# Handing out VectorE's work between pieces: attention's masked copies and transposes, the sums of x, one silu product, and the rows of the output tile

## Chip, core and metric

The kernel runs on one core of one Trainium2 chip. The metric is the device time of one execution in microseconds (us). TensorE does the matrix products, VectorE (DVE in the profile) and GpSimd (POOL) the elementwise work, ScalarE (ACT) activations and copies, and SyncE (SP) issues most of the transfers. Each engine works its own instructions in the order in which the program issues them. Between engines, semaphores hold an instruction back until what it reads has been written and what it overwrites has been read.

## What is computed

Two stages follow each other. The first is a linear attention with a decay per channel; the second is a feed-forward layer with a silu gate.

```python
for t in range(S):                                   # r, k, v: (4, 8, 768, 48)
    cur = einsum('bhd,bhe->bhde', u[None] * kt, vt)
    y[:, :, t] = einsum('bhd,bhde->bhe', rt, state + cur)
    state = w[None, :, :, None] * state + einsum('bhd,bhe->bhde', kt, vt)
x = y.transpose(0, 2, 1, 3).reshape(3072, 384)
g, val = x @ w_gate, x @ w_val                       # (3072, 1536)
out = (g * (1 / (1 + exp(-g))) * val) @ w_out        # (3072, 384)
```

## The kernel before

The sequence is cut into blocks of 128 tokens: 24 blocks (`N`), four of them (one for each batch) at every one of six places in time. Attention of block `i` is done in chunked form. `turn_blocks` puts k and r with the channel on partitions, by two VectorE transposes, first k (`kT`), then r (`rT`). Before it `move_blocks` has brought the 32x32 blocks into place by 16 transfers on SP's queue; these overwrite what the transposes of the block before read, so they wait for its second transpose. `scores` multiplies the two on TensorE for even and odd heads, and two `copy_predicated` (L392) put the upper triangles into `At`. `outputs` forms the rows of x, `update` the state. The main loop over `s` (L1036) does `scores(s-1)`, `outputs(s-2)`, `update(s-2)` and `turn_blocks(s)`; from `s = 12` on the transposes are VectorE's.

Between these parts of attention stand five gaps. In each, `feed(n)` takes `n` pieces of the feed-forward layer from the list `todo`. A piece issues a few TensorE products and the VectorE, ScalarE and GpSimd work that belongs to them. So the order of the work on every engine is written out by the program: what is issued at one place in the loop stands at one place in every engine's queue.

The feed-forward layer has two shapes after the first two pairs of blocks. Pair `g` is two blocks (256 tokens).

- `three_beside(g)`, for g = 2, 4 and 6, makes gate and value products of pairs g and g+1 with 15 products of sums where 18 plain ones would be needed. It runs over t = 0 to 3, three columns of 128 of the weights each. The 15 steps of one t are called r0 to r14 and numbered 0 to 14 in `BESIDE` (`ENDING` for t = 3); step n of t has the time 15 t + n. One step is two matmuls of 256 columns (L710). Steps collect in chains, each in a PSUM bank; a chain that is read out (L735) between two of its steps must be read before the next one adds to it. Of the six results of one t, three are gates, in rows of the tile `hv`, and three are values, in the last six rows of `hv` (`NR` and on, the same rows for every t). `silu` activates a gate (L742) and multiplies it by its value (L735, `hv<-hv`): product i = 0 and 1 of a t on VectorE early in the next t, i = 2 on GpSimd.
- `two_projections(g)` projects pairs g and g+1 with seven products of half size each, named by pair and number: "00" to "06", "10" to "16" (L529, six matmuls of 192 columns each). Before them stand sums of h (`h_sums`, L503 to L507). One of the items also issues eleven VectorE sums of x (`x_forms`, L668 to L678), which the next `three_beside` or `three_units` reads. The items come in the order 00 10 01 02 11 04 03 12 05 06 13 14 15 16. The results go to `o_sb1` and `o_sb2`, two buffers each, by copies and sums (L535 to L545), and from there to `out` by transfers that ScalarE issues (L553).

`queue` mixes the two: the first three pieces of the next `three_beside` (steps r10, r14, r12, each of which opens a chain and takes a free bank) are put between the last projections, in the order 13, r10, 14, r14, 15, r12, 16. Project "15" ends with the ScalarE copy (L539) that frees the bank which r12 takes. The last four pairs use `three_units` (g = 8 and 10), after attention.

Of the kernel before, what the change touches and what calls it, by code (L numbers as in the profile page):

```python
# [15 lines left out]
P = 128  # L16
# [6 lines left out]
def fast(  # L23
# [57 lines left out]
    NX = 10  # L81
    xT = cst.tile([P, NX, CC, P], FP32, name="xT")
    NR = 2 * FC
    hv = cst.tile([P, NR + 6, 2 * P], FP32, name="hv")
    hTs = hv[:, 0:NR].rearrange("p (j f) t -> p j f t", j=2)
    sgs = cst.tile([P, 3, 2 * P], FP32, name="sgs")
    free_sg = deque(sgs[:, n] for n in range(3))
# [287 lines left out]
    def turn_blocks(i):  # L375

        turned[i] = three.tile([P, HP, P], FP32, name="rT", tag="rT")
        for dst, src in ((kT[i % 2], blocks[0]), (turned[i], blocks[1])):
            dve.transpose(dst[:].rearrange("p a t -> p (a t)"), src)

    def scores(i):

        ps = [ps_a.tile([P, HP, P], FP32, name="s_ps", tag="a") for _ in range(2)]
        for a in range(HP):
            for e in range(2):
                rows = slice(64 * e, 64 * e + D)
                pe.matmul(  # L387
                    ps[e][:, a, :], kT[i % 2][rows, at(i, a), :], turned[i][rows, at(i, a), :],
                    start=True, stop=True, skip_group_check=True,
                )  # L390
        for e in range(2):
            dve.copy_predicated(  # L392
                At[i % 2][:].rearrange("p (a e) t -> p a e t", e=2)[:, :, e],
                mask[:].bitcast(INT32).unsqueeze(1).to_broadcast([P, HP, P]), ps[e][:],
            )

    def outputs(i):

# [110 lines left out]
    def project(g, n):  # L509

        h11, h12, h21, h22 = h_quarters(g)
        x = part_of.setdefault(g, {})
        if n == 0:
            assert done["pool"] == NW
            if g == 0:
                free.extend(banks[2:])
            x["a"] = take()
            x["out"] = [two.tile([P, DM], FP32, name=n, tag=n) for n in ("o_sb1", "o_sb2")]
        if n == 1:
            x["b"] = take()  # L520
        lhs, rhs, acc = (
            (h11, w11, "a"), (h12, w21, "b"), (1, wt[0], "a"), (2, wt[1], "a"),
            (0, w12, "b"), (h22, wt[2], "a"), (3, w22, "b"),
        )[n]
        if isinstance(lhs, int):
            lhs = x["s"][lhs]
        ps = x[acc][:, 0:NH]
        for f in range(FH):
            pe.matmul(  # L529
                ps, lhs[:, f, :], rhs[:, f, :],  # L530
                start=(f == 0 and n in (0, 1, 4)), stop=(f == FH - 1), skip_group_check=True,
            )
        o1, o2 = x["out"]
        if n in (0, 2, 3):
            act.copy({0: o1[:, 0:NH], 2: o1[:, NH:DM], 3: o2[:, NH:DM]}[n], ps)  # L535
        elif n == 1:
            dve.tensor_add(o1[:, 0:NH], o1[:, 0:NH], ps)
        elif n == 5:
            act.copy(o2[:, 0:NH], ps)  # L539
            free.append(x["a"])  # L540
        elif n == 6:
            dve.tensor_add(o1[:, NH:DM], o1[:, NH:DM], ps)  # L542
        if n in (3, 4):
            if "c22" in x:
                dve.tensor_add(o2[:, NH:DM], o2[:, NH:DM], x["b"][:, 0:NH])  # L545
            x["c22"] = True
        if n == 6:
            free.append(x["b"])
        if n >= 5:
            j = 6 - n  # L550
            c, b = divmod(2 * g + j, B)
            n0 = S * b + P * c
            act.dma_start(out=out[n0 : n0 + P, :], in_=x["out"][j][:])  # L553

# [14 lines left out]
    def two_projections(g):  # L569

        def item(j, p):
            if g >= FIRST and (j, p) == (0, 1):
                for do in wide.pop("last"):
                    do()
            if (j, p) in ((1, 0), (0, 1)):
                h_sums(g, p)
            elif (j, p) in ((1, 1), (0, 3)):
                h_sums(g + 1, p // 3)
            elif g + 2 < THREES and (j, p) == (0, 6):
                x_forms(g + 2)  # L580
# [27 lines left out]
    wide, todo_forms = {}, deque()  # L608

    def in_place(t):  # L610

# [42 lines left out]
    def x_forms(g):  # L654

        (x00, x01), (x10, x11), (x20, x21) = x_halves(g)
        lows2 = [two.tile([P, 3, 2, P], FP32, name="xf", tag="w_low") for _ in range(2)]
        v = [t[:, n] for t in lows2 for n in range(3)]
        if g < THREES:
            v += [sgs[:, n].rearrange("p (i t) -> p i t", i=2) for n in range(3)] + [x01, x10]  # L660
        else:
            last = two.tile([P, H, D], FP32, name="xf", tag="rk")
            v += [
                t.rearrange("p h d -> p (h d)")[:, 0 : 2 * P].rearrange("p (i t) -> p i t", i=2)
                for t in [x[:] for x in r_ld + k_ld] + [last[:]]
            ]
        v10, v13, v6, v2, v12, d1, v3, v1, v8, v4, v14 = v
        dve.tensor_add(v10, x01, x21)  # L668
        dve.tensor_sub(v13, x00, v10)
        dve.tensor_add(v12, v13, x20)  # L670
        dve.tensor_sub(d1, x11, x10)
        dve.tensor_sub(v2, d1, x20)
        dve.tensor_add(v6, v2, x21)
        dve.tensor_sub(v3, x00, x11)
        dve.tensor_sub(v1, x10, x00)
        dve.tensor_sub(v8, x01, x11)
        dve.tensor_sub(v4, x01, x00)
        dve.tensor_add(v14, x10, x20)  # L678
        wide["v", g] = {
            "r0": d1, "r1": v1, "r2": v2, "r3": v3, "r4": v4, "r5": x00, "r6": v6, "r7": x21,  # L680
            "r8": v8, "r9": x20, "r10": v10, "r11": x11, "r12": v12, "r13": v13, "r14": v14,
        }

    def prepare_threes(g, n):
        if g >= THREES and n == 10:
            x_forms(g)
        if g > THREES:
            return
        if n == 1:
            if g == FIRST:  # L690
# [34 lines left out]
    def three_beside(g):  # L725

        todo = []
        values = hv[:, NR : NR + 6].rearrange("p (j i) t -> p j i t", j=2)

        def pair_of(x):  # L730
            return x.rearrange("p (o t) -> p o t", o=2)
# [13 lines left out]
        for t in range(4):  # L745
# [8 lines left out]
            if t < 3:  # L754
                forms = w_forms(g, t + 1)
                if g == FIRST and t < 2:
                    forms += in_place(t + 2)
                start = z - 4 if t else 0
                todo += [
                    (start + (z + 10 - start) * n / len(forms) + 0.15, do)  # L760
                    for n, do in enumerate(forms)
                ]
            gates = [[j * FC + 3 * t + i for i in range(3)] for j in range(2)]
            c = []
            for k in range(6):
                i, j = divmod(k, 2)
                row, other = gates[j][i], NR + 3 * j + i
# [30 lines left out]
            if t < 3:  # L798
                for i, on in enumerate((dve, dve, pool)):
                    silu(  # L800
                        *((z + 11.7, z + 11.8) if i == 2 else (z + 15.6 + i / 10, z + 16.2 + i / 10)),
                        hTs[:, :, 3 * t + i], values[:, :, i], on,
                    )
            else:
# [99 lines left out]
    def feed(n, pops=1):  # L904
        for _ in range(n):
            ready = [k for k, (need, _) in enumerate(todo) if need <= done["pool"] + len(summed)]
            if ready:
                todo.pop(ready[0])[1]()
            for _ in range(min(pops, len(small))):
                small.popleft()()  # L910

    def queue(g):
# [5 lines left out]
        elif g % 2 and g > 1:  # L918
# [593 lines left out]
```

## Time and profile before

| what | value |
|---|---|
| median of 3 runs | 608.4 us (608.32 to 608.64) |
| the profiled execution | 608.25 us |
| its span (first to last instruction) | 606.5 us |
| TensorE busy | 587.9 us (97% of the span) |
| VectorE busy | 408.4 us (67%) |
| GpSimd busy | 311.6 us (51%) |
| ScalarE busy | 228.2 us (38%) |
| mean granted TensorE clock | 0.999 |

The span and the time differ by 1.75 us, which lie outside the first and the last instruction. The busy share of TensorE counts matmuls to their modelled ends, which overlap: matmuls of 256 columns start 0.216 us apart and are shown about 0.38 us long. A step of `three_beside` (four rows in the records, since each fp32 matmul appears twice) therefore takes 0.86 us, and one of the seven products of a projection (12 rows) 1.95 us; a wait is best read as what two starts lie apart beyond that.

### The profile page before, as it was taken

What the parts mean: (1) busy time and instruction counts of PE and PEld (TensorE: products, weight loads), DVE (VectorE), ACT (ScalarE), POOL (GpSimd) and SP (SyncE); (2) the same over time, 40 slices, a digit from 0 to 9 for tenths busy, and PEclk for the clock granted to TensorE, in tenths of its full rate; (3) what the DMA queues carried; (4) which work ended last, traced back from release to release, by engine and by line L of the source; (5) the groups of instructions that cost most, each with busy time, mean ns of one, the idle gap of its engine ahead of it and who ended that gap; (6) DMA issues with size and microseconds to landing.
All of it is one profiled execution on the core that took longest, in us unless ns stands there. A gap on an engine that the chain in (4) does not pass through costs nothing.

```text
span 606.5 us, 12429 instructions
## 1 busy us (share of the span) xinstructions
PE 587.9 (97%) x4920; PEld 527.2 (87%) x4920; DVE 408.4 (67%) x682; ACT 228.2 (38%) x524; POOL 311.6 (51%) x349
## 2 busy tenths in 40 slices
PE   8799999999999999999999999999999999999996
PEld 7588888899888899888799988889888899988896
DVE  6767877369478876478778377868537674377660
ACT  3358887330453422154331233432233420243310
POOL 4779879988999402967701866632435300001000
PEclk9999999999999999999999999999999999999999
DMA  6979883241530503133151404131100000100001
GB/s 168 237 210 245 221 294 77 46 70 31 123 49 9 93 5 72 42 60 56 21 85 21 96 3 67 19 51 24 37 17 1 1 0 19 35 1 1 2 1 57
DMA packets 138004, 40.43 MB, mean 67 GB/s; under 512 B 128592, under 2 KB 131792, under 8 KB 137936
## 3 DMA queue, kind: packets, MB, share of 16 engines
q1 hardware_dynamic: 134480, 34.82, 27.2%
q10 hardware_dynamic: 3456, 4.72, 2.2%
q8 instruction: 41, 0.67, 0.5%
q14 instruction: 27, 0.22, 0.1%
HBM read 28.51 MB, written 4.72 MB: 55 GB/s over the span
## 4 chain that ended last, share of the span: by engine, by line
PE 83%; DVE 4%; POOL 3%; ACT 2%; issue 1%; DMA 1%; ACTq 0%; DVEq 0%; SPq 0%; POOLq 0%
PE bank L710 27%; PE bank L529 26%; PE bank L455 7%; PE c_l L710 6%; PE y_ps L417 5%; PE c_n L710 3%; PE c_y L710 3%; PE s_ps L387 3%; DVE hv L735 2%; POOL wgv L222 1%; PE u_ps L432 1%; PE tp L349 1%; DMA r_ld<-in_r_dram 1%; ACT hv L735 1%; ACT hv L742 1%
## 5 line engine op out<-in xcount | busy, mean ns | idle before, releaser
L735 DVE TENSOR_TENSOR hv<-hv,bank 128x512 f32<-128x512 f32 x132 | 87.5, 681 | 29.8 <-PE bank L710 16.8
L455 PE MATMUL bank<-xT,wgv 128*128 128x256 f32 x288 | 66.8, 385 | 0.6 <-ACT xT L421 0.6
L710 PE MATMUL bank<-xf,wgv 128*128 128x256 f32 x256 | 65.9, 382 | 1.1 <-ACT o_sb L539 1.1
L328 ACT ACTIVATE At<-ident,du 128x128 f32<-128x128 f32 x176 | 60.1, 396 | 14.8 <-DVE o_sb L542 6.9
L849 POOL TENSOR_TENSOR hv<-At,hats 128x512 f32<-128x512 f32 x8 | 10.2, 1274 | 107.0 <-ACT At L848 107.0
L735 ACT COPY hv<-bank 128x512 f32<-128x512 f32 x72 | 40.3, 585 | 58.2 <-PE bank L710 43.4
L455 PEld LDWEIGHTS bank<-xT,wgv 128*128 128x128 f32 x288 | 53.2, 190 | 8.9 <-ACT xT L421 0.8
L710 PEld LDWEIGHTS bank<-xf,wgv 128*128 128x128 f32 x256 | 48.0, 190 | 8.6 <-ACT o_sb L539 1.8
L642 POOL TENSOR_TENSOR s<-wgv 128x256 f32<-128x256 f32 x39 | 29.3, 773 | 43.3 <-PE bank L529 43.3
L529 PE MATMUL bank<-wo,hv 128*128 128x192 f32 x288 | 49.5, 327 | 0.0
L529 PEld LDWEIGHTS bank<-wo,hv 128*128 128x128 f32 x288 | 47.3, 190 | 0.5
L392 DVE COPY_PREDICATED At<-mask,s_ps 128x512 f32<-128x512 int32 x48 | 33.1, 744 | 19.1 <-ACT At L328 10.5
L445 POOL TENSOR_TENSOR Z<-Z,w 48x192 f32<-48x192 f32 x32 | 17.3, 540 | 53.3 <-DVE Z L444 52.0
L529 PE MATMUL bank<-wo,hs 128*128 128x192 f32 x240 | 42.5, 327 | 1.2 <-DVE o_sb L545 1.2
L529 PE MATMUL bank<-wt,hs 128*128 128x192 f32 x240 | 42.1, 328 | 0.1
L535 ACT COPY o_sb<-bank 128x192 f32<-128x192 f32 x36 | 11.3, 315 | 80.2 <-PE bank L529 70.6
L529 PEld LDWEIGHTS bank<-wo,hs 128*128 128x128 f32 x240 | 39.6, 190 | 1.9 <-DVE o_sb L545 1.5
L529 PEld LDWEIGHTS bank<-wt,hs 128*128 128x128 f32 x240 | 39.2, 190 | 1.1 <-issue 0.7
L710 PE MATMUL bank<-xT,s 128*128 128x256 f32 x152 | 36.4, 383 | 2.5 <-DVE hv L735 2.0
L742 ACT ACTIVATE hv<-hv 128x512 f32<-128x512 f32 (+1 forms) x33 | 21.2, 668 | 45.2 <-DVE hv L735 45.2
L417 PE MATMUL y_ps<-At,v_ld 128*32 128x128 f32 x768 | 34.9, 273 | 1.4 <-DVE At L392 1.4
L710 PE MATMUL bank<-xT,wgv 128*128 128x256 f32 x144 | 35.9, 382 | 0.0
(212 smaller groups left out, 1302.0 us busy)
## 6 DMA issues: line engine op xcount, KB each, us to landing
hats<-hats SPq DMA_DIRECT2D x192, 32.0 KB, 2.0
w_bits<-in_moe_w_gate_dram SPq DMA_DIRECT2D x6, 768.0 KB, 6.7
v_ld<-in_v_dram SPq DMA_DIRECT2D x48, 96.0 KB, 3.5
w_bits<-in_moe_w_val_dram SPq DMA_DIRECT2D x6, 768.0 KB, 6.1
w_bits<-in_moe_w_out_dram SPq DMA_DIRECT2D x6, 768.0 KB, 7.1
out_dram<-o_sb ACTq DMA_DIRECT2D x24, 192.0 KB, 1.9
k_ld<-in_k_dram SPq DMA_DIRECT2D x20, 192.0 KB, 3.4
r_ld<-in_r_dram SPq DMA_DIRECT2D x20, 192.0 KB, 3.8
```

The lines of the kernel that those rows point to most:

```text
L328: lambda h=h: act.activation(At[i % 2][:, h, :], ident[:], AF.Identity, scale=du[:, h : h + 1])
L387: pe.matmul(ps[e][:, a, :], kT[i % 2][rows, at(i, a), :], turned[i][rows, at(i, a), :], start=True, stop=True, skip_group_check=True,)
L392: dve.copy_predicated(At[i % 2][:].rearrange("p (a e) t -> p a e t", e=2)[:, :, e], mask[:].bitcast(INT32).unsqueeze(1).to_broadcast([P, H ...
L417: pe.matmul(ps[32 * q : 32 * q + 32, cc, :], *x, start=start, stop=stop, skip_group_check=True,)
L445: pool.tensor_mul(ze, ze, w)
L455: pe.matmul(gv[:, o, :].rearrange("p (i t) -> p i t", i=2), wt[:, c, P * f : P * (f + 1)], xT[:, 2 * g % NX : 2 * g % NX + 2, c, :], start ...
L529: pe.matmul(ps, lhs[:, f, :], rhs[:, f, :], start=(f == 0 and n in (0, 1, 4)), stop=(f == FH - 1), skip_group_check=True,)
L535: act.copy({0: o1[:, 0:NH], 2: o1[:, NH:DM], 3: o2[:, NH:DM]}[n], ps)
L642: op(made[o], made[a], made[b])
L710: pe.matmul(ps[:, o], u[:, o], v, start=first and o == 0, stop=True, skip_group_check=True,)
L735: do(out, *(pair_of(wide[a][:]) if isinstance(a, str) else a for a in args))
L742: todo.append((at, lambda: act.activation(gate, gate, AF.Silu)))
```

## The change

1. Of the two masked copies of `scores`, for blocks from 12 on, only the first is issued at once. The second is put in a list `lazy`, and the next `feed` issues it behind its first piece.
2. `turn_blocks` issues one piece between the transpose of k and that of r. To make up for it the gap ahead of it (gap 1) feeds one piece less.
3. The eleven sums of x are made into a list, two of which go into each of six items of `two_projections`, from "03" to "14" (before: all eleven in item "06" or, for the sums of pairs 8 and on, "13"). Their order changes a little.
4. Product i = 1 of t = 0 and 1 is issued at step 7.1 of the next t instead of 1.3.
5. The values of t = 1 go into six new rows of `hv`. These rows are also the output tile: `o_sb1` and `o_sb2` are gone, and each pair's results go to three of the six rows.
6. Two instead of three pieces of the next `three_beside` go between the last projections: 13, r10, 14, r14, 15, 16, r12.

No instruction is added or removed on any engine. On TensorE the order differs only by item 6, in three places.

```diff
-    hv = cst.tile([P, NR + 6, 2 * P], FP32, name="hv")
+    hv = cst.tile([P, NR + 12, 2 * P], FP32, name="hv")
...
         for dst, src in ((kT[i % 2], blocks[0]), (turned[i], blocks[1])):
             dve.transpose(dst[:].rearrange("p a t -> p (a t)"), src)
+            if dst is kT[i % 2]:
+                feed(1)
+    lazy = deque()
     def scores(i):
+        while lazy:
+            lazy.popleft()()
...
         for e in range(2):
-            dve.copy_predicated(
+            lazy.append(lambda e=e: dve.copy_predicated(
...
+        lazy.popleft()()
+        if i < BLOCKS:
+            lazy.popleft()()
...
-            x["out"] = [two.tile([P, DM], FP32, name=n, tag=n) for n in ("o_sb1", "o_sb2")]
+            rows = hv[:, NR + 6 + 3 * (g % 2) : NR + 9 + 3 * (g % 2)].rearrange("p r t -> p (r t)")
+            x["out"] = [rows[:, DM * k : DM * k + DM] for k in range(2)]
...
-        dve.tensor_add(v10, x01, x21)
-        dve.tensor_sub(v13, x00, v10)
...
+        todo_x.extend(
+            lambda out=out, a=a, b=b, op=op: op(out, a, b) for out, a, b, op in (
+                (v10, x01, x21, dve.tensor_add), (v13, x00, v10, dve.tensor_sub),
...
     def prepare_threes(g, n):
-        if g >= THREES and n == 10:
+        if n == 6:
             x_forms(g)
+        for _ in range(2):
+            if todo_x:
+                todo_x.popleft()()
...
+            place = NR + (6 if t == 1 else 0)
+            values = hv[:, place : place + 6].rearrange("p (j i) t -> p j i t", j=2)
...
-                        *((z + 11.7, z + 11.8) if i == 2 else (z + 15.6 + i / 10, z + 16.2 + i / 10)),
+                        *((z + 11.7, z + 11.8) if i == 2 else (z + 15.6 + i / 10, z + (22.1 if i and t < 2 else 16.2 + i / 10))),
...
     def feed(n, pops=1):
         for _ in range(n):
             ready = [k for k, (need, _) in enumerate(todo) if need <= done["pool"] + len(summed)]
             if ready:
                 todo.pop(ready[0])[1]()
+            if lazy:
+                lazy.popleft()()
...
-            for k in range(3):
+            for k in range(2):
                 others.insert(len(others) - 3 + k, pieces.pop(0))
...
-            feed(share[0] // 5 + (n < share[0] % 5))
+            feed(share[0] // 5 + (n < share[0] % 5) - (n == 1 and BLOCKS <= s < N))
```

More of the change, by code (lines that the diff above doesn't have):

```diff
@@ L391, in scores @@
         for e in range(2):
-            dve.copy_predicated(
+            lazy.append(lambda e=e: dve.copy_predicated(
                 At[i % 2][:].rearrange("p (a e) t -> p a e t", e=2)[:, :, e],
                 mask[:].bitcast(INT32).unsqueeze(1).to_broadcast([P, HP, P]), ps[e][:],
-            )
+            ))
+        lazy.popleft()()
+        if i < BLOCKS:
+            lazy.popleft()()
     def outputs(i):
@@ L552, in project @@
             n0 = S * b + P * c
-            act.dma_start(out=out[n0 : n0 + P, :], in_=x["out"][j][:])
+            act.dma_start(out=out[n0 : n0 + P, :], in_=x["out"][j])
     def x_halves(g):
@@ L578, in item @@
                 h_sums(g + 1, p // 3)
-            elif g + 2 < THREES and (j, p) == (0, 6):
-                x_forms(g + 2)
             if g + 2 < N // 2:
@@ L607, in fast @@
     early += [flat[:, 256 * n : 256 * n + 256] for n in range(2)]
-    wide, todo_forms = {}, deque()
+    wide, todo_forms, todo_x = {}, deque(), deque()
     def in_place(t):
@@ L667, in x_forms @@
         v10, v13, v6, v2, v12, d1, v3, v1, v8, v4, v14 = v
-        dve.tensor_add(v10, x01, x21)
-        dve.tensor_sub(v13, x00, v10)
[L670 to L678, printed above, removed]
+        todo_x.extend(
+            lambda out=out, a=a, b=b, op=op: op(out, a, b) for out, a, b, op in (
+                (v10, x01, x21, dve.tensor_add), (v13, x00, v10, dve.tensor_sub),
+                (v12, v13, x20, dve.tensor_add), (d1, x11, x10, dve.tensor_sub),
+                (v2, d1, x20, dve.tensor_sub), (v6, v2, x21, dve.tensor_add),
+                (v1, x10, x00, dve.tensor_sub), (v14, x10, x20, dve.tensor_add),
+                (v3, x00, x11, dve.tensor_sub), (v8, x01, x11, dve.tensor_sub),
+                (v4, x01, x00, dve.tensor_sub),
+            )
+        )
         wide["v", g] = {
@@ L727, in three_beside @@
         todo = []
-        values = hv[:, NR : NR + 6].rearrange("p (j i) t -> p j i t", j=2)
         def pair_of(x):
@@ L766, in three_beside @@
                 i, j = divmod(k, 2)
-                row, other = gates[j][i], NR + 3 * j + i
+                row, other = gates[j][i], place + 3 * j + i
                 low, high = hv[:, row], hv[:, other]
```

## Prediction

> **What bounds the kernel now.** I read the page first. TensorE is busy for 97% of the span at full granted clock, so nothing that another engine does counts unless it makes TensorE wait.
>
> ```profile
> PE 587.9 (97%) x4920; PEld 527.2 (87%) x4920; DVE 408.4 (67%) x682; ACT 228.2 (38%) x524; POOL 311.6 (51%) x349
> PEclk9999999999999999999999999999999999999999
> ```
>
> TensorE's own waits come next. The rows with warm, tp, kT, xT and the larger y_ps one lie in the first 60 us, where this change alters nothing (for blocks under 12 both masked copies are still issued at once). After them four kinds are left.
>
> ```profile
> PE bank L710 <- DVE hv L735: 2.0, 2, 1.3
> PE bank L529 <- DVE o_sb L545: 1.2, 1, 1.2
> PE bank L710 <- ACT o_sb L539: 1.1, 3, 0.4
> PE bank L710 <- ACT hv L735: 0.3, 1, 0.3
> ```
>
> They look small because idle time counts from the modelled end of the last matmul. Starts tell the loss better: 0.86 us for a step, 1.95 us for a product of a projection. To know which step a row is I counted the L710 rows by fours. The timeline shows the largest loss, step r5 of t = 3 in g = 4.
>
> ```profile
> 298.59 2.94 DVE L735 TENSOR_TENSOR hv<-hv 128x512 f32<-128x512 f32 x2 [0.78 <-ACT hv L742]
> 301.45 0.70 DVE L379 STREAM_TRANSPOSE kT<-hats 128x512 f32<-128x512 f32 x1
> 302.08 0.66 DVE L379 STREAM_TRANSPOSE rT<-hats 128x512 f32<-128x512 f32 x1
> 302.67 1.84 DVE L735 TENSOR_TENSOR hv<-hv,bank 128x512 f32<-128x512 f32 x3
> ```
>
> ```profile
> 300.94 1.10 PE L710 MATMUL bank<-xT,s 128*128 128x256 f32 x4
> 303.37 1.56 PE L710 MATMUL bank<-xT,s 128*128 128x256 f32 x6 [1.33 <-DVE hv L735]
> ```
>
> Two silu products and two transposes stand in VectorE's queue ahead of the sum that reads r13's chain, and r5 must not add to that chain before. 303.37 - 300.94 - 0.86 is 1.57 us, and the step that restarts takes 0.10 longer. So VectorE is not short of time (67%); it is late at certain places. By the same count all waits of TensorE on other engines after 60 us cost about 9 us with their restarts. That is the most the change can win.
>
> **The change part by part.**
>
> Losses that should go:
>
> A. r12 behind "16" (item 6). In g = 4 ScalarE's copy (L539) begins at 249.58 and r12 waits for it:
>
> ```profile
> 249.58 0.32 ACT L539 COPY o_sb<-bank 128x192 f32<-128x192 f32 x1 [1.36 <-PE bank L529]
> 249.95 0.70 PE L710 MATMUL bank<-xf,wgv 128*128 128x256 f32 x2 [0.41 <-ACT o_sb L539]
> ```
>
> "15" ends its issue at 249.38, so 0.57 is lost and 0.10 with the restart. "16" needs no new bank and covers the copy with 1.95 us. Three places (155, 250, 342 us): 0.45 + 0.67 + 0.67 = 1.8 us. r12's own copy comes 1.95 us later; r9 needs it three steps after r12 starts (2.6 us), and it ends after about 1.65 (0.86, 0.2, 0.59).
>
> B. The sums of x spread out (item 3). "16" of g = 6 (start 438.43) came 3.30 us after "15" instead of 1.95; it waits for the last row here:
>
> ```profile
> 431.81 0.70 DVE L668 TENSOR_TENSOR xf<-xT 128x256 f32<-128x256 f32 x1
> ...
> 437.69 0.42 DVE L678 TENSOR_TENSOR xf<-xT 128x256 f32<-128x256 f32 x1
> 438.03 0.35 DVE L545 TENSOR_TENSOR o_sb<-o_sb,bank 128x192 f32<-128x192 f32 x1
> ```
>
> In the new order only three of the eleven stand behind "06", and they are done before "14", whose result that sum reads, ends at 435.1. Gain 1.35 + 0.10 = 1.45 us. The first two now stand ahead of the earlier L545 sum, which "06" waits for: 2 x 0.42 to 2 x 0.95 from 422.7 on make it end at 425.0 at the latest, and "06" starts at 426.32. In g = 0 the same slack is 0.8 us, in g = 4 1.7. Hidden there; without that slack each would cost up to 1 us.
>
> C. One silu product later (item 4). At t = 0 to 1 of g = 6 r5 started 1.65 us after r9 (365.02 - 363.37). Without product 1 (cadence 1.13) and with the k transpose ahead of product 0, r13's sum ends near 363.4 instead of 365.0, and r5 is due at 364.23: 0.79 + 0.10 = 0.9 us won. At 1 to 2 the values' new rows (item 5) also let ScalarE's copy of r10 go without waiting for GpSimd's product (189.89 and 280.97 in its rows): 0.3 + 0.2 = 0.5 us.
>
> D. The place shown above is t = 2 to 3, whose products stay where they were. There only the k transpose moves ahead of them, into the 0.78 us in which VectorE waited for ScalarE; the second masked copy now uses 0.65 us just before, but fits into gaps of 0.2 between sums. r13's sum starts about 0.6 us earlier: 0.6 won, about 1.0 stays.
>
> Costs that come instead:
>
> E. The k transpose is issued right after gap 1, ahead of what stood before it. In g = 2 that is the sums of h for "02" (L503, L504), and "02" was already late:
>
> ```profile
> 222.59 0.95 DVE L503 TENSOR_TENSOR hs<-hv 128x768 f32<-128x768 f32 x1
> 223.57 0.96 DVE L504 TENSOR_TENSOR hs<-hs,hv 128x768 f32<-128x768 f32 x1
> 224.45 0.70 DVE L379 STREAM_TRANSPOSE kT<-hats 128x512 f32<-128x512 f32 x1
> ```
>
> That adds 0.65 us; "04", which waited 0.1 itself, gives some of it back: 0.5 us lost.
>
> F. In g = 6, t = 3, the transpose of block 22 moves from 403.23 to behind r5's sum and the second masked copy, 401.1. It reads what SP's 16 transfers bring:
>
> ```profile
> 399.31 1.26 SPq L364 DMA_DIRECT2D hats<-hats  x2
> 400.67 1.10 SPq L128 DMA_DIRECT2D v_ld<-in_v_dram  x2
> 404.59 0.61 SPq L364 DMA_DIRECT2D hats<-hats  x1
> ```
>
> The last is issued at 399.97 and a transfer of this row lands in 2.0 us (page, part 6), so at 401.9; the r transpose of block 21, which starts this chain, comes 0.25 us later than before, so 402.2. Queued behind the waiting transpose are the sums that read r1, r3 and r6 (before: 400.82, 401.76, 402.62). r0 adds to r1's chain and is due at 402.35; r1's sum now ends at 402.2 + 0.65 + 0.67 = 403.5. Lost: 1.2, with the restart 1.3 us. At ten of the other transposes the data land 5 us or more ahead, at block 23 0.8 us.
>
> G. The late products themselves. At step 7.1 they stand between r5's sum and r6's sum. A product takes 0.69 to 1.53 us in this trace (18 of `hv<-hv` 128x512): about 0.7 in the shortest rows, 1.2 to 1.5 beside GpSimd's L642 and L234 rows. The Trainium skill speaks against this move: "SBUF — State Buffer", "Who interferes with whom", says that a DVE instruction with two SBUF inputs contends with a GpSimd instruction that reads SBUF, and that who starts first holds the pair for a whole instruction. In g = 2, t = 2, the product would start at 196.2 amid L642 rows. By the rule it pays a whole 0.73 us more, r6's sum ends at 198.4 and r7, due 198.20, waits 0.2; by the shortest rows there is no wait. The other five places have attention between r11 and r7, or an idle GpSimd. With the rule this term is 0.3 us and the whole gain 3.15; with the shortest rows 0 and 3.45. I take 0.1, since a product there may also start first.
>
> At nothing: the output rows (item 5). The same two buffers take turns; the first write of t = 1 into them (360.2 in g = 6) comes 14 us after the last output transfer is issued (345.98), which lands in 1.9; without that cover a wait of up to 1.9 on ScalarE. The second masked copy later: `outputs` reads its tile a step of s later, over 10 us. The r transpose behind a piece: SP's 16 transfers, the loads of v and, for even s, of k and r stand behind it. The largest delay is in g = 4, where four sums and a masked copy come between (330.4 to about 334): landing near 346.5, read at 361; if that cover were gone, 3.5 us. Elsewhere SP waits for GpSimd's L310 anyway (252.00). The queues of POOL and SP keep their order but for one POOL row.
>
> Sum: 1.8 + 1.45 + 0.9 + 0.5 + 0.6 - 0.5 - 1.3 - 0.1 = 3.35 us. From the profiled execution's 608.25 that gives 604.9; the median of the runs is 0.15 above that execution, so 605.0.
>
> **The rivals.**
>
> 1. ScalarE takes over. Behind C and D stands its chain of copy, silu, silu, copy; it delayed r2 by about 0.2 at six places already. If C and D give nothing (2.0 less), 607.0. Against: in g = 6, t = 1, the y copy ends at 362.3, before r2 at 362.51.
> 2. No new waits: E and F do not come, since an earlier TensorE or shorter chain leaves slack. Then 1.8 more: 603.2. Against: F's landing time does not hang on TensorE.
> 3. Slower: the transposes ahead of sums. Each of twelve k transposes is put 1 to 3 sums earlier, 0.65 us each on an in-order queue. If all twelve found TensorE without slack, 12 x 0.65 + 0.6 (F's wait for landing) = 8.4 against 5.25 won: 608.4 + 3.15 = 611.5. It decides from eight transposes on the path; I count two. For it: VectorE is 80% filled within a group (0.69 of 0.86 per step). Against: the sums moved lie mostly one or more steps ahead of the step that needs them.
> 4. No effect: the waits are passed on one for one to later ones, 608.4. Against: after each loss TensorE runs steps at 0.86 us with no debt.
>
> **How the numbers follow.** Forecast 605.0, chance 0.58, own range 603.8 to 606.2. Rival 1: 0.17. Rival 2: 0.14. Rival 4: 0.06. Rival 3: 0.05. A measurement of this kernel can tell about 0.2%, 1.2 us. Faster by more than that (under 607.2): the forecast, rival 2 and nearly all of rival 1, 0.88. Within: rival 4 and the edge of 1, 0.08. Slower: 0.04. The range 603.0 to 606.9 takes rival 2 and most of rival 1.
>
> **What would show it.** No `<-ACT o_sb L539` in TensorE's waits (A); no wait on L545's successor (B); r5 of g = 6, t = 1 0.86 after r9 (C); about 1 us before r5 in g = 4, t = 3 (D); a DVE row that waits for DMA `hats<-hats`, and a TensorE wait near 400 us on the sum behind it (F); 0.7 before "02" in g = 2 (E). TensorE's waits after 60 us should fall from about 9 to about 6 us. Wrong if transposes wait for transfers at more than one block, or new TensorE waits on `hv` or `xf` appear.

## The result and the profile after

The median went from 608.36 us (607.81 to 610.02, 14 runs) to 605.33 us (604.50 to 608.17, 14 runs). The ratio is 0.9954, with a 95% interval of 0.9941 to 0.9968. The prediction had 605.0, with a range of 603.8 to 606.2. The profiled execution took 605.01 us, its span is 603.2. TensorE's row and its clock on the page of the changed kernel:

```profile
PE 587.1 (97%) x4920; PEld 528.0 (88%) x4920; DVE 405.6 (67%) x682; ACT 228.2 (38%) x524; POOL 313.3 (52%) x349
...
PEclk9999999999999999999999999999999999999999
```

The busy shares are those of before: no work went away. What changed stands in TensorE's waits (engine, line, what it waited for: us in total, times, longest). After 60 us these rows are left. L720 and L744 are the steps and their sums (before L710 and L735), L539 the projections, L513 the second sum of h (before L504).

```profile
PE bank L720 <- DVE hv L744: 2.5, 2, 1.7
...
PE bank L539 <- DVE hs L513: 0.6, 1, 0.6
...
PE bank L720 <- ACT hv L744: 0.2, 1, 0.2
```

Two rows are gone: the three waits on ScalarE's copy ahead of r12 and the wait on the sum ahead of "16". One row is new, on the sums of h. The row on VectorE has grown although one of its two waits of before is gone and the other has shrunk (before 0.62 and 1.33 of idle time, r5 of g = 6, t = 1 and of g = 4, t = 3), so a new one must be in it.

The timeline shows each place (a row's `xN` counts its records: four to a step, twelve to a product of a projection). At the end of the projection of g = 2, "16" now covers the copy (L549), and r12 starts 1.95 us after it:

```profile
248.73 2.11 PE L539 MATMUL bank<-wo,hs 128*128 128x192 f32 x12
248.93 0.32 ACT L549 COPY hv<-bank 128x192 f32<-128x192 f32 x1 [1.36 <-PE bank L539]
250.68 1.03 PE L720 MATMUL bank<-xf,wgv 128*128 128x256 f32 x4
```

In g = 6 the sum that "16" reads waits for TensorE, where before it stood behind eleven sums of x, and "16" follows "15" after 1.95:

```profile
433.22 2.11 PE L539 MATMUL bank<-wt,hv 128*128 128x192 f32 x12
433.49 0.35 DVE L555 TENSOR_TENSOR hv<-hv,bank 128x192 f32<-128x192 f32 x1 [1.86 <-PE bank L539]
435.17 2.11 PE L539 MATMUL bank<-wo,hs 128*128 128x192 f32 x12
```

At t = 0 to 1 of g = 6 two products and two transposes stood ahead of r13's sum before, and r5 came 1.65 us after r9 (363.37):

```profile
361.32 1.86 DVE L735 TENSOR_TENSOR hv<-hv 128x512 f32<-128x512 f32 x2 [0.78 <-ACT hv L742]
363.10 0.70 DVE L379 STREAM_TRANSPOSE kT<-hats 128x512 f32<-128x512 f32 x1
365.02 1.35 PE L710 MATMUL bank<-xT,s 128*128 128x256 f32 x5 [0.62 <-DVE hv L735]
```

Now one product and one transpose are left there, and r5 follows r9 (360.61) without a gap:

```profile
358.51 0.80 DVE L744 TENSOR_TENSOR hv<-hv 128x512 f32<-128x512 f32 x1
359.23 0.70 DVE L379 STREAM_TRANSPOSE rT<-hats 128x512 f32<-128x512 f32 x1
360.61 1.67 PE L720 MATMUL bank<-xT,s 128*128 128x256 f32 x7
```

At t = 2 to 3 of g = 4 the k transpose has left the place behind the two products. They still take 2.96 us, and r5 comes 1.83 us after r9 (2.43 before):

```profile
296.30 0.71 DVE L379 STREAM_TRANSPOSE kT<-hats 128x512 f32<-128x512 f32 x1
297.07 2.96 DVE L744 TENSOR_TENSOR hv<-hv 128x512 f32<-128x512 f32 x2
299.96 0.70 DVE L379 STREAM_TRANSPOSE rT<-hats 128x512 f32<-128x512 f32 x1
300.58 1.84 DVE L744 TENSOR_TENSOR hv<-hv,bank 128x512 f32<-128x512 f32 x3
...
299.45 1.10 PE L720 MATMUL bank<-xT,s 128*128 128x256 f32 x4 [0.17 <-ACT hv L744]
301.28 1.99 PE L720 MATMUL bank<-xT,s 128*128 128x256 f32 x8 [0.73 <-DVE hv L744]
```

And the two places that the change made worse. In g = 2 the transpose is ahead of the sums of h, and "02" waits:

```profile
221.44 0.70 DVE L379 STREAM_TRANSPOSE kT<-hats 128x512 f32<-128x512 f32 x1
222.07 0.92 DVE L512 TENSOR_TENSOR hs<-hv 128x768 f32<-128x768 f32 x1
223.02 0.96 DVE L513 TENSOR_TENSOR hs<-hs,hv 128x768 f32<-128x768 f32 x1
...
224.13 2.19 PE L539 MATMUL bank<-wt,hs 128*128 128x192 f32 x12 [0.62 <-DVE hs L513]
```

In g = 6, t = 3, VectorE stands idle for 1.84 us before the k transpose of block 22, whose data are on their way. Behind it are the three sums that TensorE needs, and r0 waits:

```profile
396.41 0.74 DVE L398 COPY_PREDICATED At<-mask,s_ps 128x512 f32<-128x512 int32 x1
398.99 0.71 DVE L379 STREAM_TRANSPOSE kT<-hats 128x512 f32<-128x512 f32 x1 [1.84 <-DMA hats<-hats]
399.62 1.85 DVE L744 TENSOR_TENSOR hv<-hv,bank 128x512 f32<-128x512 f32 x3
400.33 1.13 PE L720 MATMUL bank<-xf,wgv 128*128 128x256 f32 x4 [1.72 <-DVE hv L744]
```

**A finer ruler than the median.** TensorE works the same steps in almost the same order in all these kernels. So the start of a named step in one trace can be set against its start in another, and the difference put down to the stretch in which it arose. Stretches that an edit doesn't touch agree to 0.02 us, except the one with the landing (F). There the changed kernel's own second trace is 0.18 longer than its first, and four others whose edits don't touch it differ from the first by -0.22 (sums of x at once), 0.02 and 0.23 (product early, second and first) and 0.74 (product early with shared rows, whose clock fell as well; see the last section). The table has, for every stretch between two starts, how much longer (+) or shorter (-) it is than in the changed kernel's first trace. The columns are the kernel before and experiments told below.

| stretch, up to the start of | before | turns together | two turns old | r turn early | x at once | product early (2nd) | both masks | third product |
|---|---|---|---|---|---|---|---|---|
| r13 of g = 2, t = 0 (A) | 0.36 | 0.00 | 0.01 | 0.01 | 0.01 | 0.00 | 0.00 | 0.01 |
| r9 of g = 2, t = 2 (C) | 0.35 | 0.00 | 0.00 | 0.00 | 0.00 | 0.01 | 0.01 | 0.00 |
| "03" of g = 2 (E) | -0.51 | -0.49 | -0.49 | 0.00 | 0.01 | 0.17 | 0.00 | -0.90 |
| r13 of g = 4, t = 0 (A) | 0.68 | -0.01 | 0.00 | 0.00 | 0.00 | 0.00 | -0.01 | -0.01 |
| r5 of g = 4, t = 2 (C) | 0.20 | 0.14 | 0.00 | 0.00 | -0.01 | 0.12 | 0.00 | 0.01 |
| r11 of g = 4, t = 3 (D) | 0.57 | 0.58 | 0.00 | 0.00 | 0.00 | 0.07 | 0.00 | -0.99 |
| r13 of g = 6, t = 0 (A) | 0.67 | -0.01 | 0.00 | 0.00 | -0.01 | 0.00 | -0.01 | 0.00 |
| r11 of g = 6, t = 1 (C) | 0.89 | 0.00 | 0.00 | 0.00 | 0.00 | 0.37 | 0.00 | 0.00 |
| r11 of g = 6, t = 3 | 0.26 | 0.36 | 0.00 | 0.28 | 0.00 | 0.00 | -0.25 | 0.00 |
| r4 of g = 6, t = 3 (F) | -1.99 | -1.98 | -1.99 | -1.90 | -0.22 | 0.02 | -0.49 | -1.96 |
| r14 of g = 8, t = 0 (B) | 1.44 | -0.01 | 0.00 | -0.02 | 1.66 | -0.02 | -0.01 | -0.01 |
| from "00" of g = 0 to the last r4 | 2.92 | -1.42 | -2.47 | -1.63 | 1.45 | 0.75 | -0.76 | -3.85 |

The first column is the change, place by place: 2.92 us, beside 3.03 between the medians. The spans of the two profiled executions lie 3.3 us apart; 0.44 of that arises before "00" of g = 0, where the traces differ by waits for the first loads of k, r and v from one execution to the next.

The two rows of g = 6, t = 3 belong together. Where r0 waits for the landing, the landing sets its start: what TensorE wins or loses just ahead of it (the upper row) is given back in the lower one. Together they are -1.73 for the kernel before, -1.62 with the transposes together and -0.74 with both masks.

### The profile page after: what moved, and what is told of

It reads as the page before. It is cut to its first block, busy times and chain, and to the rows that moved or that the text cites. A ratio compares the mean times of both kernels' runs of the same rounds, so it can differ in the third digit from the quotient of the medians.

```text
span 603.2 us, 12420 instructions
## 1 busy us (share of the span) xinstructions
PE 587.1 (97%) x4920; PEld 528.0 (88%) x4920; DVE 405.6 (67%) x682; ACT 228.2 (38%) x524; POOL 313.3 (52%) x349
## 4 chain that ended last, share of the span: by engine, by line
PE 83%; DVE 3%; POOL 3%; SPq 2%; ACT 1%; issue 1%; DMA 1%; DVEq 0%; POOLq 0%; ACTq 0%
PE bank L720 27%; PE bank L539 26%; PE bank L464 7%; PE c_l L720 6%; PE y_ps L426 5%; PE c_n L720 3%; PE c_y L720 3%; PE s_ps L393 3%; DVE hv L744 2%; SPq L364 2%; POOL wgv L222 1%; PE u_ps L441 1%; PE tp L349 1%; DMA r_ld<-in_r_dram 1%; ACT hv L751 0%
## 5 line engine op out<-in xcount | busy, mean ns | idle before, releaser
L744 DVE TENSOR_TENSOR hv<-hv,bank 128x512 f32<-128x512 f32 x132 | 87.2, 682 | 30.5 <-PE bank L720 17.6
L720 PE MATMUL bank<-xf,wgv 128*128 128x256 f32 x256 | 65.9, 381 | 1.7 <-DVE hv L744 1.7
L744 ACT COPY hv<-bank 128x512 f32<-128x512 f32 x72 | 40.2, 585 | 55.2 <-PE bank L720 49.1
L720 PEld LDWEIGHTS bank<-xf,wgv 128*128 128x128 f32 x256 | 48.0, 190 | 8.9 <-DVE hv L744 2.1
L650 POOL TENSOR_TENSOR s<-wgv 128x256 f32<-128x256 f32 x39 | 29.7, 785 | 43.8 <-PE bank L539 43.7
L539 PE MATMUL bank<-wo,hv 128*128 128x192 f32 x288 | 49.5, 327 | 0.0
L539 PEld LDWEIGHTS bank<-wo,hv 128*128 128x128 f32 x288 | 47.3, 190 | 0.5
L539 PE MATMUL bank<-wt,hs 128*128 128x192 f32 x240 | 42.1, 328 | 0.7 <-DVE hs L513 0.6
L539 PE MATMUL bank<-wo,hs 128*128 128x192 f32 x240 | 42.4, 326 | 0.0
L545 ACT COPY hv<-bank 128x192 f32<-128x192 f32 x36 | 11.3, 316 | 78.6 <-PE bank L539 78.6
L539 PEld LDWEIGHTS bank<-wt,hs 128*128 128x128 f32 x240 | 39.2, 190 | 1.7 <-issue 1.3
L539 PEld LDWEIGHTS bank<-wo,hs 128*128 128x128 f32 x240 | 39.6, 190 | 0.2
L720 PE MATMUL bank<-xT,s 128*128 128x256 f32 x152 | 36.0, 382 | 1.0 <-DVE hv L744 0.7
L720 PE MATMUL bank<-xT,wgv 128*128 128x256 f32 x144 | 35.9, 382 | 0.0
```

The lines of the kernel that those rows point to most:

```text
L539: pe.matmul(ps, lhs[:, f, :], rhs[:, f, :], start=(f == 0 and n in (0, 1, 4)), stop=(f == FH - 1), skip_group_check=True,)
L650: op(made[o], made[a], made[b])
L720: pe.matmul(ps[:, o], u[:, o], v, start=first and o == 0, stop=True, skip_group_check=True,)
L744: do(out, *(pair_of(wide[a][:]) if isinstance(a, str) else a for a in args))
```

## The experiments

**Part A alone**, in the kernel before:

```diff
-            for k in range(3):
+            for k in range(2):
                 others.insert(len(others) - 3 + k, pieces.pop(0))
```

> The kernel before with one edit of the change: only r10 and r14 are put ahead of the late products of the projection, so that r12 follows "16". Theory (part A of the prediction): the three waits of TensorE on ScalarE's copy ahead of r12 (0.10, 0.57 and 0.57 us lost, each with 0.10 for the restart) vanish, 1.7 to 1.8 us in all: 606.6 against 608.4. Rival (the waits are handed on to a later step one for one): 608.4, with new waits of about the same size within five steps of r12.

Measured: 606.31 us, ratio to before 0.9974 (0.9965 to 0.9982), that is 1.78 us less on the same chip (608.09). By places it wins 0.35, 0.69 and 0.67 and all others stay as before. Two rows of its waits: the one on L539 is gone, the one on L545 stays.

```profile
PE bank L710 <- DVE hv L735: 1.9, 2, 1.3
...
PE bank L529 <- DVE o_sb L545: 1.2, 1, 1.2
```

The gain stands by itself and is not handed on.

**The transposes together again**, in the changed kernel:

```diff
             dve.transpose(dst[:].rearrange("p a t -> p (a t)"), src)
-            if dst is kT[i % 2]:
-                feed(1)
...
-            feed(share[0] // 5 + (n < share[0] % 5) - (n == 1 and BLOCKS <= s < N))
+            feed(share[0] // 5 + (n < share[0] % 5))
```

> The changed kernel with both transposes of every block issued together again, after the second gap, as before the change. Theory (each place counted by itself): E comes back (0.5), F comes back (2.0 as the changed kernel's trace has it: 1.89 and the restart), D is lost again (0.6): 605.3 - 2.5 + 0.6 = 603.4; no wait ahead of "02" in g = 2 beyond 0.2 and none ahead of r0 of t = 3 in g = 6. Rival 1 (the early k transpose also carries C, because it no longer stands between the products and r13's sum): r5 of t = 1 in g = 6 waits again by 0.7 or so, 604.1. Rival 2 (the transposes ahead of the sums are what wins): slower than the changed kernel, 606.5 or more.

Measured: 603.52 us, ratio to before 0.9929 (0.9916 to 0.9941). E and F go, D comes back, and r2 of t = 3 in g = 6 and of t = 2 in g = 4 lose a little, all in the table's second column. So item 2 of the change, taken as a whole, is a loss of 1.4 us by places: it wins 0.58 where it was needed and 0.14 at r2 of t = 2 in g = 4, and pays 0.49 and 1.62 in two places where nothing was to be won (the 0.36 at r2 of t = 3 in g = 6 goes into the wait that follows). Rival 1 falls: r5 of t = 1 in g = 6 doesn't wait without the early transpose either.

**Two transposes in the old place.**

```diff
-            if dst is kT[i % 2]:
+            if dst is kT[i % 2] and i not in (15, 22):
                 feed(1)
...
- (n == 1 and BLOCKS <= s < N))
+ (n == 1 and BLOCKS <= s < N and s not in (15, 22)))
```

> The changed kernel with the k transposes of two blocks only, 15 (end of g = 2) and 22 (t = 3 of g = 6), back behind the sums they were moved ahead of; all else as changed. Theory: E and F vanish and nothing else moves: "02" of g = 2 loses 0.2 instead of 0.79, r0 of t = 3 in g = 6 nothing instead of 1.89, each with its restart: 605.3 - 0.5 - 2.0 = 602.8. Rival (at block 22 TensorE has run so far ahead that it waits for something else there, ScalarE's copy or the landing of the r block): the 2.0 stay, 604.8.

Measured: 602.68 us, ratio to before 0.9910 (0.9897 to 0.9923). The timeline of block 22 shows why nothing is handed on. The sums come first, each as soon as TensorE has the step behind it, and the transpose starts 0.67 us after its data landed at 398.56, with no one waiting:

```profile
396.94 1.50 DVE L744 TENSOR_TENSOR hv<-hv,bank 128x512 f32<-128x512 f32 x2
398.62 0.69 DVE L744 TENSOR_TENSOR hv<-hv,bank 128x512 f32<-128x512 f32 x1 [0.17 <-PE bank L720]
399.23 0.70 DVE L379 STREAM_TRANSPOSE kT<-hats 128x512 f32<-128x512 f32 x1
```

**The r transpose of block 21 early**, so that the transfers for block 22 start earlier; the place of the k transpose stays as changed:

```diff
-            if dst is kT[i % 2]:
+            if dst is (turned[i] if i == 21 else kT[i % 2]):
                 feed(1)
```

> The changed kernel with one edit: at block 21 the r transpose follows the k transpose at once, so that SP's sixteen transfers for block 22 start earlier. Theory (F is set by the landing of those transfers): they start 1.9 us earlier (at 384.5 instead of 386.4), land near 396.9 instead of 398.8, and the wait ahead of r0 of t = 3 in g = 6 falls from 1.89 to 0.1 or less: 603.4 to 603.5. The sums behind the r transpose come 0.6 later, which may cost 0.1 to 0.3. Rival (the queue is held by something else, GpSimd's product behind the same block or the k transpose's place alone): the landing stays at 398.8 and so does the wait, 605.3.

Measured: 603.61 us, ratio to before 0.9933 (0.9920 to 0.9946). VectorE's rows:

```profile
384.10 0.67 DVE L379 STREAM_TRANSPOSE rT<-hats 128x512 f32<-128x512 f32 x1
...
397.06 0.73 DVE L398 COPY_PREDICATED At<-mask,s_ps 128x512 f32<-128x512 int32 x1
397.73 0.71 DVE L379 STREAM_TRANSPOSE kT<-hats 128x512 f32<-128x512 f32 x1
```

The transfers were issued from 384.83 and had landed at 397.51. Counted from the start of "00", they start 1.96 us earlier than in the changed kernel and land 1.6 earlier, since the sixteen took 0.35 longer. It was enough: no idle time stands before the transpose, and r0 comes in its turn. The sums behind the r transpose cost 0.28 at r2 and r9 of the same t. F is the landing, and what the landing hangs on is when the r transpose of the block before is issued.

**The sums of x at once** (the list stays, but is emptied where the sums stood before):

```diff
-        if n == 6:
+        if n == (10 if g >= THREES else 9):
             x_forms(g)
-        for _ in range(2):
-            if todo_x:
+            while todo_x:
                 todo_x.popleft()()
```

> The changed kernel with the eleven sums of x of a group issued in one go again, at the places before the change (behind "06" of the projection, for g = 8 behind "13"). Theory (part B): "16" of g = 6 starts 3.3 us after "15" again instead of 1.95, 1.35 and 0.10 for the restart: 605.3 + 1.45 = 606.8. Rival (with the k transposes and masked copies of the changed kernel VectorE has other slack there, and the sums are done in time): 605.3.

Measured: 607.27 us, ratio to before 0.9984 (0.9974 to 0.9994). "16" comes 3.52 us after "15", 0.2 more than before the change (the eleven stand in the changed kernel's new order):

```profile
435.58 0.72 DVE L398 COPY_PREDICATED At<-mask,s_ps 128x512 f32<-128x512 int32 x1
436.19 0.34 DVE L555 TENSOR_TENSOR hv<-hv,bank 128x192 f32<-128x192 f32 x1
...
436.58 2.22 PE L539 MATMUL bank<-wo,hs 128*128 128x192 f32 x12 [1.41 <-DVE hv L555]
```

The second masked copy, which item 1 has moved, now stands in that queue too. B is the spreading of the sums, and 1.66 us would be lost without it.

**Product 1 early again**, with and without the new rows:

```diff
-z + (22.1 if i and t < 2 else 16.2 + i / 10)
+z + 16.2 + i / 10
```

> The changed kernel with silu product 1 of every t back behind product 0; the values of t = 1 stay in the output tile's rows, the k transposes where the change put them. Theory 1 (as the prediction's part C has it, the late product wins r5 of t = 1 in g = 6): the 0.9 us come back, 606.2. Theory 2 (formed after the run with both transposes together, in which this wait stayed away too: one of the two edits is enough): r13's sum starts 0.7 us later than in the changed kernel, at 360.7 on its time, and ends at 361.4, just when r5 is due (361.48): 0 to 0.1 us lost, 605.3 to 605.4.

> The changed kernel with silu product 1 of every t back behind product 0, and the values of all t in the same six rows again (items 4 and the values' part of 5 undone). Theory: beside what the early product alone does, r2 of t = 2 waits again for the copies of r10 and r14 that wait for GpSimd's product: 0.19 in g = 2 and 0.15 in g = 4 with restarts of 0.10, 0.4 to 0.5 us more than with the early product alone. Rival (the rows are worth nothing, the copies wait for ScalarE's own chain): the same time as with the early product alone.

The first gave 607.36 us, ratio to before 0.9983 (0.9972 to 0.9994), the second 606.98 (0.9976; 0.9966 to 0.9986). Neither theory on r5 of t = 1 in g = 6 held: 0.37 us come back, not 0.9 and not 0. The four corners show how the two edits share it: neither edit 0.89 (before, and part A alone, which lack the rest of the change too), early transpose alone 0.37, late product alone 0 (transposes together), both 0. What the second theory got wrong is the product's length. I took 0.7 us; it takes 1.22 (two products take 1.93, the second starts 0.72 after the first). That is not this place alone: behind product 0 it took 1.21 or 1.22 in all six places before the change, beside different rows of GpSimd. Here they are L650 and L310, and the one of L310 takes 1.45 where others take 1.0:

```profile
358.82 1.93 DVE L744 TENSOR_TENSOR hv<-hv 128x512 f32<-128x512 f32 x2
360.68 0.70 DVE L379 STREAM_TRANSPOSE rT<-hats 128x512 f32<-128x512 f32 x1
361.30 1.84 DVE L744 TENSOR_TENSOR hv<-hv,bank 128x512 f32<-128x512 f32 x3
...
360.17 1.45 POOL L310 TENSOR_TENSOR hats<-r_ld,scales 128x384 f32<-128x384 f32 x1
```

As for the rows: with the six shared again, r2 of t = 2 in g = 2 waits as before (0.36 in that stretch) and in g = 4 by 0.12 more, 0.48 as expected; 0.2 to 0.3 of it is won back in later stretches, and the medians, if anything, stand the other way round. This run's profiled execution (608.18 us) is also 2.2 us longer behind r11 of t = 3 in g = 6, where the edit changes nothing; the last section has what stands there. By places the rows are worth about what was expected; by time this is unclear.

**The changed kernel and product 1 early on one chip**, since the medians above had them 2 us apart and the places 0.6 to 0.9:

> The changed kernel itself, beside the two that follow and the kernel before on one chip, as the base for them: product 1 early was 1.3 to 2.0 us slower in its median than the changed kernel measured on another chip, while its places add up to 0.6 (0.36 and its restart before r5 of t = 1 in g = 6, 0.2 more before r0 of t = 3). Theory 1 (the places are the whole difference, the rest is chip and clock): 605.9 to 606.3 here. Theory 2 (the late product wins something that the places do not show): 605.3 again.

> The changed kernel with silu product 1 of every t back behind product 0, on the same chip as the changed kernel. Theory 1 (the places are the whole difference): 0.6 us above it. Theory 2: 1.3 us or more above it.

Measured: 605.93 us (0.9971; 0.9960 to 0.9982) and 607.38 us (0.9982; 0.9968 to 0.9996). That is 1.45 between medians, while the traces differ by 0.57 over the places (446.27 and 445.70 from "00" to the last r4). The single runs say more than the medians: those with a mean granted clock of 0.997 or more have medians of 605.60 and 605.67, and six of the nine runs of the early product were below that clock, five of the fourteen of the changed kernel. So theory 1 stands by the traces. That the rest is the clock is likely, since one trace shows what a stretch of lower clock costs (last section), but for these two sets of runs it is not shown. It also tells the limit of the method: less than 1 us is read from places here, not from medians.

**Both masked copies at once** (item 1 undone):

```diff
         lazy.popleft()()
-        if i < BLOCKS:
-            lazy.popleft()()
+        lazy.popleft()()
```

> The changed kernel with item 2 undone: both masked copies of a block are issued at once, as before. Theory (the second copy costs nothing in either place): VectorE has an idle stretch of 0.5 us or more behind or ahead of most of the first copies (350.9, 380.4, 392.5 on the changed kernel's time), so the same time within 0.3 us, and the same waits of TensorE. Rival (the second copy at once stands ahead of a sum that TensorE waits for): 0.65 us or more slower, with a new wait behind a masked copy.

The text on record says item 2; the edit undoes item 1. Measured: 604.88 us, ratio to before 0.9956 (0.9941 to 0.9972), 1.05 below the changed kernel on that chip, and 0.76 less by places. Both theories missed: it is faster. The rows of block 21 and 22:

```profile
384.43 0.69 DVE L743 TENSOR_TENSOR hv<-hv,bank 128x512 f32<-128x512 f32 x1
385.03 0.68 DVE L743 TENSOR_TENSOR hv<-bank,hv 128x512 f32<-128x512 f32 x1
385.63 0.70 DVE L379 STREAM_TRANSPOSE rT<-hats 128x512 f32<-128x512 f32 x1
...
398.82 0.71 DVE L379 STREAM_TRANSPOSE kT<-hats 128x512 f32<-128x512 f32 x1 [2.00 <-DMA hats<-hats]
```

In the changed kernel a masked copy stands between those two sums and the r transpose:

```profile
385.05 0.73 DVE L398 COPY_PREDICATED At<-mask,s_ps 128x512 f32<-128x512 int32 x1
```

Counted from the start of "00", the r transpose comes 0.63 us earlier without it, the first transfer 0.62 and the landing 0.74 (the sixteen took 0.12 less, which lies within their scatter). r0 comes 0.75 earlier; 0.25 of that shows already at r2 and r9 of t = 3, behind the same transpose.

**One more late product**, with the two transposes old: product 1 of t = 2 too, its two values in rows of t = 1 that are free by then:

```diff
-row, other = gates[j][i], place + 3 * j + i
+row, other = gates[j][i], (NR + 6 + 3 * j if (t, i) == (2, 1) else place + 3 * j + i)
...
-z + (22.1 if i and t < 2 else 16.2 + i / 10)
+z + (22.1 if i else 16.2)
...
-hTs[:, :, 3 * t + i], values[:, :, i], on,
+hTs[:, :, 3 * t + i],
+spare_values[:, :, 0] if (t, i) == (2, 1) else values[:, :, i], on,
```

> The changed kernel with the transposes of blocks 15 and 22 in their old place (602.7) and one edit more: product 1 of t = 2 is issued seven steps later too; its two values' rows are two rows of t = 1 whose product is done by then. Theory: what stays before r5 of t = 3 in g = 4 (0.89 and the restart) is that product, 0.7 us on VectorE: r13's sum starts 0.7 us earlier, 0.2 stays; the 0.30 and 0.10 before r5 of t = 3 in g = 2 go as well: 602.7 - 0.7 - 0.4 = 601.6, at best 601.5. Rival (behind it stands ScalarE's chain of copy, silu, silu, copy, which already delays r9 there by 0.33): r13's sum starts no earlier than its copy allows, 602.4 or more.

Measured: 601.54 us, ratio to before 0.9880 (0.9857 to 0.9902). It beats both kernels. TensorE's wait on VectorE's `hv` is gone altogether, and at the place where the prediction began there is one product where two stood:

```profile
297.97 1.57 DVE L744 TENSOR_TENSOR hv<-hv 128x512 f32<-128x512 f32 x1
299.46 0.70 DVE L379 STREAM_TRANSPOSE rT<-hats 128x512 f32<-128x512 f32 x1
300.08 1.24 DVE L744 TENSOR_TENSOR hv<-hv,bank 128x512 f32<-128x512 f32 x2
```

The same with all transposes together asks what the early transpose is worth then:

> The kernel with the late product at t = 2 too (601.5 with only the turns of blocks 15 and 22 in the old place), but with every k transpose back beside its r transpose. It asks what the early k transpose is worth once the product is late. Theory (each place counted): at r5 of t = 3 in g = 4 the transpose returns ahead of r13's sum and brings 0.6, of r2 of t = 3 in g = 6 0.35, of r2 of t = 2 in g = 4 0.13: 602.6. Rival (the late products leave VectorE enough slack that the transposes' place no longer matters): 601.5.

Measured: 602.48 us (0.9899; 0.9885 to 0.9913). By places it is 0.64 behind: 0.12 at r2 of t = 2 in g = 4, 0.17 at r5 of t = 3, 0.35 at r2 of t = 3 in g = 6. The late product does most of what the early transpose did at r5 (0.17 is left of 0.6). Whether both masked copies at once add to the best version was not tried.

## Why the prediction was right

- **A**: 1.8 expected, 1.71 measured, and 1.71 alone. No `<-ACT o_sb L539` is left, as said.
- **B**: 1.45 expected, 1.44 measured.
- **C**: 0.9 at r5, measured 0.89; 0.5 at the two r2, measured 0.55. The size was right. The cause was half right: the late product is enough by itself, and the early transpose, which the working named beside it, isn't needed. It alone would have won 0.52 of the 0.89.
- **D**: 0.6 expected, 0.57 measured; r5 starts 0.97 after it was due (about 1.0 was to stay).
- **E**: 0.5 lost, as expected (0.51); "02" waits 0.79 by starts, where 0.7 was named.
- **F**: 1.3 expected, 1.73 measured. In its own stretch r0 loses 1.99, but 0.26 of that is what TensorE had won just ahead of it (r9 of t = 3 no longer waits 0.44, r2 waits 0.15 instead), and the landing takes it back. The place, the wait on `hats<-hats` and the chain behind it were right; the size of this term was not. Against the sum, VectorE starts 0.23 us after the landing, where the sum had it start at once, and SP's chain from first issue to landing took 12.33 us instead of 12.13; together 0.43. The second part is scatter: over all fourteen traces the chain takes 12.1 to 12.9 us.
- **The second masked copy, at nothing**: this step of the working failed. It had seen that the r transpose of block 21 comes 0.25 later (0.24 measured), but asked of the masked copy only when its tile is read. The copy also stands ahead of the r transpose, and with it of SP's transfers. Issued at once it would have saved 0.76 us by places, 0.62 of it by the earlier first transfer.
- **G**: 0.1 expected, nothing measured. No r7 waits. At g = 2, t = 2, where the Trainium skill ("SBUF — State Buffer", "Who interferes with whom") let one expect a whole instruction more, the product took 0.68 us, and GpSimd's row beside it paid: 1.28 instead of 0.73. The page states the hold for a whole instruction where it speaks of VectorE's two-port modes; of two SBUF inputs it states that the two contend, and with that this trace agrees: here GpSimd was the one that lost.

The sum of the measured terms is 1.71 + 1.44 + 0.89 + 0.55 + 0.57 - 0.51 - 1.73 = 2.92, against 3.35. Nearly all of the difference is F. Of the two signs of being wrong neither came: one transpose waits for its transfers (`DVE kT L379 <- DMA hats<-hats: 1.8, 1, 1.8`), and the only new wait of TensorE on `hv` is the one that F forecast.

Of the rivals, the first (ScalarE takes over) would have shown C and D without effect; they have theirs. The second (no new waits) is refuted by E and F, though the kernel comes to 602.68 when these two are taken out, near that rival's 603.2. The third counted transposes on the path: they are the two that were counted, not eight. Yet its direction was right for the transposes alone, which cost 1.4 more than they won, as the forecast's own D, E and F had it (0.6 - 0.5 - 1.3). The fourth is refuted by part A alone.

## What to carry to other kernels

When an in-order engine is late at one place, move what stands before it at that place alone: a rule for all twelve blocks (the k transpose one piece earlier) was paid at the two where its data or its neighbour's were just in time. Whatever is moved ahead of an instruction that starts a chain of transfers delays their landing too, so ask of each neighbour that is passed who waits for it, the queues included. And where a program runs the same named steps in every version, compare the starts of steps stretch by stretch: it shows 0.1 us where medians show 1, as long as the clock is the same and no transfer's landing lies in the stretch.

## What the runs showed of the hardware

- VectorE begins a transpose that waits for a transfer 0.21 to 0.23 us after the last landing in the trace (398.76 to 398.99, 398.61 to 398.82, and 399.58 to 399.80 in the second run of the changed kernel).
- Of a VectorE product of two SBUF tiles and a GpSimd row that reads SBUF beside it, one pays, and which one differs by place. At 195.02 in the changed kernel VectorE's product took 0.68 us, and GpSimd's rows are:

```profile
193.52 0.73 POOL L650 TENSOR_TENSOR s<-s,wgv 128x256 f32<-128x256 f32 x1
194.20 0.73 POOL L650 TENSOR_TENSOR s<-s 128x256 f32<-128x256 f32 x1
195.01 1.28 POOL L650 TENSOR_TENSOR s<-s,wgv 128x256 f32<-128x256 f32 x1
```

  GpSimd's row, recorded as starting 0.01 us before the product, ends 0.59 after it. In the best version the same pair starts 0.01 apart again (196.81 and 196.80), and there VectorE pays: its product takes 1.25 us, GpSimd's row 0.73. So the recorded starts do not tell which one will.

  Before the change product 1 of t = 0 and 1 took 1.21 or 1.22 us in all six places, directly behind another product. Seven steps later it took 0.68 or 0.69 in four, 1.11 and 1.31 in two. So moving it also saved VectorE some 2 us of busy time, which the prediction had not counted.
- TensorE's waits for the first loads of k, r and v ranged from 1.7 us (the changed kernel's first trace) to 4.6 us (the best version's). "00" of g = 0 starts between 123.75 and 125.74.
- Apart from about the first and the last 9 us, the granted clock was full throughout eleven of the fourteen traces, and fell to half once, for 3.41 us, in the other three. In product 1 early with shared rows this came at 402.67, 0.74 us behind the wait that F causes (2.26 us of idle time there, 1.72 in the changed kernel's first trace). The page shows it as an 8:

```profile
PEclk9999999999999999999999999989999999999999
```

  From r0 of t = 3 in g = 6 to r14 of g = 8 TensorE took 1.68 us longer there than in the trace of product 1 early. In the best version and with both masks at once the fall came near 28 us, 2.0 and 2.2 us behind a wait of 2.15 and 2.00. One wait of 2.04 (16.44 in the best version) was not followed by one before the next wait, and none of the waits up to 1.95 us in the fourteen traces was. So an execution with a long wait can lose more than the wait itself; what decides when it does is not shown.
